# Retention followed by mixture of depths: when the second and third batch's tokens are chosen, and how the first MLPs are dealt out to the steps

## Chip, cores, metric

One core of one Trainium2 chip. The metric is the device time of one execution in microseconds; the runs of the kernel before took 259.76 us in the median of three (258.28 to 263.15).

## The reference, cut to what matters

All arrays are float32. There are 8 batches of 8 heads, 576 positions and head size 64, so a token has 512 channels; the MLP has 1024 hidden units and each batch sends its 128 best tokens through it.

```python
scores = scale * np.matmul(q, k.transpose(0, 1, 3, 2))
gamma = 1.0 - 2.0 ** (-5.0 - np.arange(H))
Dmat = np.where(rel >= 0, gamma[:, None, None] ** rel[None, :, :], 0.0)
x = np.matmul(scores * Dmat, v)                 # to (B, S, H*D)
s = np.einsum('bsd,d->bs', x, w_gate)
out = x.copy()
for b in range(B):
    top_idx = np.argpartition(-s[b], capacity)[:capacity]
    xe = x[b, top_idx]
    ye = np.maximum(xe @ w1, 0.0) @ w2
    g = 1.0 / (1.0 + np.exp(-s[b, top_idx]))
    out[b, top_idx] = xe + g[:, None] * ye
```

## The kernel before

**Steps.** A batch has nine chunks of 64 positions. Two chunks make a page of q, k (both turned), v and k, 1 MB in four transfers, and there are 36 pages. Turn s of the main loop works on page s: `block(s)` writes to TensorE's queue the products of k and q of page s (`scores`, L184), the running state (`update`, L174, which reads `vs`, v scaled by the decay) and, for page s-1, the outputs (`crosswise`, L195 and L205, which reads the masked scores `am` of page s-1). A state update of the page's own first chunk stands in the last quarter of the block's order, and the outputs of page s-1 are dealt two by two between the other products, so a wait for `vs` or `am` stops everything behind it. `masked(s)` (VectorE, L260) then makes `am`, `values(s-1)` (VectorE, L269 and L278) the outputs and their gate scores, and `store(s-1)` (GpSimd queue, L286) writes them to memory. `scaled(s+1)` makes the next `vs`: on GpSimd (L160, one instruction), or on ScalarE (L156, eight) where `by_act` says so, and for page 12 on VectorE.

**Choosing tokens.** A batch ends with a page; `ends[b]` is the step in which its last values are made: 5, 9, 14, 18, 23, 27, 32, 36. After it, `total` (TensorE L311, ScalarE L315) sums a token's scores, `spread` (TensorE L326, ScalarE L331) lays them in a row on all partitions, five `compare` (VectorE L339) count for each token those ahead of it (its rank), `one_hot` (VectorE L352) turns ranks into a selection, `rows` (TensorE L360, ScalarE L363) turns that into row numbers, and `gather` (GpSimd L369) fetches the 128 rows from the output in memory. `turn` (TensorE L395, ScalarE L396) transposes them, `gates` (VectorE L386, ScalarE L387) makes the sigmoid. 

**The MLP** is cut into 16 parts: eight `up` (TensorE L404, ReLU on ScalarE L406) and eight `down` (TensorE L412), the last of which adds the result to the tokens (VectorE L417) and scatters them (GpSimd L418). `mlp(b)` appends the parts of a batch to a list, and `some(n)` issues the next n of it.

**The order is written out by hand.** Every engine runs its instructions in the order of the program. `plan` puts a call into one of the lists `mid`, `early` or `late` of a step. In a step the order is: `scaled(s+1)`, `block(s)`, `masked(s)`, list `mid`, `values(s-1)`, stores, list `early`, then `some(share[s])`, then list `late`. `share` is how many parts a step gets from the loop; it is computed from `start`, the steps in which the MLPs of the batches begin.

**Loads.** SP's queue brings pages and weights in program order, with four to six transfers in flight (`bring`, L92). In step 7 it is given, in this order: the first half of w1, page 9, the second half of w1, page 10, the first half of w2 (`lower`), pages 11 and 12, the second half of w2, pages 13 and 14. There are eight page buffers.

## Time and profile before

| what | value |
|---|---|
| median of the runs | 259.76 us (258.28 to 263.15) |
| the profiled execution, its own time | 259.35 us |
| its span, first to last instruction | 257.6 us |
| TensorE matmuls busy | 222.1 us (86%) |
| TensorE weight loads busy (beside the matmuls) | 174.4 us (68%) |
| VectorE, ScalarE, GpSimd busy | 130.4, 73.1, 96.5 us |
| mean TensorE clock granted | 0.985 |
| DMA | 56.56 MB, 220 GB/s over the span |
| chain that ended last, by engine | TensorE 61%, DMA 23%, issue 11% |

In the profile, PE is TensorE's matmuls, PEld its weight loads, DVE VectorE, ACT ScalarE, POOL GpSimd and SP the engine that issues the loads. L184 is line 184 of the kernel. "Issue" as a releaser means that the engine waited for nothing that the profile shows. A bracket behind a row of the timeline is the idle time before it and what ended that. A float32 matmul leaves two records, so an up part is 8 records and a down part 2.

### The profile page before, as it was taken

How to read it: one execution, taken by the hardware profiler on the slowest of the kernel's cores; microseconds unless marked ns; L12 is line 12 of the kernel's file. 1: busy time of each engine (PE TensorE's matmuls, PEld its weight loads, DVE VectorE, ACT ScalarE, POOL GpSimd, SP SyncE). 2: the span in 40 equal slices, each digit the busy share in tenths (PEclk: the TensorE clock that was granted, in tenths of full speed). 3: DMA queues.
4: the chain of work that ended last, by engine and by line, in shares of the span. 5: the costliest groups of instructions: out<-in, count | busy, mean ns of one | idle time of the engine just before them, and what ended most of it. 6: DMA issues, size and time to landing. Idle time of an engine off the chain costs nothing.

```text
span 257.6 us, 11547 instructions
## 1 busy us (share of the span) xinstructions
PE 222.1 (86%) x5147; PEld 174.4 (68%) x5147; DVE 130.4 (51%) x355; ACT 73.1 (28%) x255; POOL 96.5 (37%) x132
## 2 busy tenths in 40 slices
PE   0875775897884999999999799999999999999991
PEld 0864564894563797689758796698669966874950
DVE  0164795339543359358535396569235774650201
ACT  2121563322011145133412234235122442221200
POOL 4313811181173460843175514550546422301101
PEclk9999999999799899999999999999999999999999
DMA  5887988989999988887889977998323304201101
GB/s 190 271 272 235 314 305 289 343 290 403 296 303 340 294 266 276 249 316 266 255 294 296 323 244 238 349 305 291 116 46 101 68 5 125 74 11 41 41 0 41
DMA packets 28097, 56.56 MB, mean 220 GB/s; under 512 B 4112, under 2 KB 4240, under 8 KB 28048
## 3 DMA queue, kind: packets, MB, share of 16 engines
q1 hardware_dynamic: 23184, 42.19, 49.9%
q0 software_dynamic: 4864, 13.64, 16.3%
q8 instruction: 40, 0.66, 1.1%
q14 instruction: 9, 0.07, 0.1%
HBM read 44.28 MB, written 11.53 MB: 217 GB/s over the span
## 4 chain that ended last, share of the span: by engine, by line
PE 61%; DMA 23%; issue 11%; ACT 1%; POOLq 1%; SPq 1%; POOL 0%; ACTq 0%
DMA raw<-in_qkvk 19%; PE h_ps L404 18%; PE ye_ps L412 18%; PE sc_ps L184 8%; PE u_ps L174 7%; DMA w_sb<-in_w 4%; PE y_ps L195 3%; PE y_ps L205 3%; PE row_ps L326 2%; PE xg_ps L395 1%; SPq L92 1%; ACT vs L156 1%; PE rs_ps L311 1%; POOLq L602 1%; PE idx_ps L360 1%
## 5 line engine op out<-in xcount | busy, mean ns | idle before, releaser
L260 DVE TENSOR_TENSOR am<-sc_ps,table 128x512 f32<-128x512 f32 x36 | 24.9, 690 | 80.6 <-PE sc_ps L184 65.8
L404 PEld LDWEIGHTS h_ps<-xg,w_sb 128*128 128x128 f32 x512 | 59.9, 193 | 6.5 <-issue 4.4
L404 PE MATMUL h_ps<-xg,w_sb 128*128 128x128 f32 x512 | 62.8, 279 | 1.3 <-ACT xg L396 0.7
L412 PE MATMUL ye_ps<-w_sb,hT 128*128 128x512 f32 x128 | 61.9, 617 | 0.2 <-issue 0.2
L184 PE MATMUL sc_ps<-raw 64*64 64x64 f32 x1152 | 47.2, 227 | 14.6 <-DMA raw<-in_qkvk 8.5
L184 PEld LDWEIGHTS sc_ps<-raw 64*64 64x64 f32 x1152 | 41.2, 141 | 16.5 <-DMA raw<-in_qkvk 8.6
L286 POOL DMA_DIRECT2D out<-xs x64 | 39.2, 620 | 31.0 <-DVE xs L269 30.8
L214 ACT COPY st<-u_ps 128x256 f32<-128x256 f32 x64 | 23.8, 371 | 93.5 <-PE u_ps L174 49.2
L174 PE MATMUL u_ps<-vs,raw 64*64 64x64 f32 x1024 | 44.6, 228 | 5.0 <-ACT st L214 3.0
L195 PE MATMUL y_ps<-vs,am 64*64 64x64 f32 x1152 | 46.8, 226 | 2.1 <-issue 1.4
L174 PEld LDWEIGHTS u_ps<-vs,raw 64*64 64x64 f32 x1024 | 37.2, 140 | 12.5 <-issue 4.9
L160 POOL TENSOR_TENSOR vs<-raw,table 128x512 f32<-128x512 f32 x27 | 28.3, 1049 | 39.9 <-DMA raw<-in_qkvk 39.6
L205 PE MATMUL y_ps<-st,raw 64*64 64x64 f32 x1024 | 39.0, 223 | 4.9 <-issue 4.9
L195 PEld LDWEIGHTS y_ps<-vs,am 64*64 64x64 f32 x1152 | 39.4, 137 | 3.4 <-issue 2.3
L339 DVE SCALAR_TENSOR_TENSOR scr<-row,rs,ahead 128x576 f32<-128x576 f32 (+5 forms) x47 | 34.2, 727 | 8.9 <-ACT row L331 6.2
L205 PEld LDWEIGHTS y_ps<-st,raw 64*64 64x64 f32 x1024 | 35.0, 139 | 5.3 <-issue 5.3
L412 PEld LDWEIGHTS ye_ps<-w_sb,hT 128*128 128x128 f32 x128 | 23.0, 194 | 21.4 <-issue 20.1
L278 DVE SCALAR_TENSOR_TENSOR scr<-xs,table 128x256 f32<-128x256 f32 x72 | 31.0, 430 | 2.5
L406 ACT ACTIVATE hT<-h_ps 128x128 f32<-128x128 f32 x64 | 17.5, 276 | 45.1 <-PE h_ps L404 43.1
L369 POOL DMA_INDIRECT xr<-out,idx x8 | 8.1, 1016 | 55.6 <-ACT idx L363 55.6
L269 DVE TENSOR_TENSOR xs<-y_ps,table 128x512 f32<-128x512 f32 (+1 forms) x37 | 24.7, 667 | 5.6 <-PE y_ps L205 5.6
L418 POOL DMA_INDIRECT out<-o,idx x8 | 9.5, 1186 | 25.8 <-DVE o L417 24.8
(38 smaller groups left out, 108.9 us busy)
## 6 DMA issues: line engine op xcount, KB each, us to landing
raw<-in_qkvk SPq DMA_DIRECT2D x144, 256.0 KB
out<-xs POOLq DMA_DIRECT2D x64, 128.0 KB, 5.2
w_sb<-in_w SPq DMA_DIRECT2D x16, 256.0 KB
out<-xs POOLq DMA_DIRECT2D x16, 64.0 KB, 4.8
table<-in_consts SPq DMA_DIRECT2D x1, 234.5 KB
xr<-out,idx POOLq DMA_INDIRECT x8, 4.3
out<-o,idx POOLq DMA_INDIRECT x8, 3.0
```

Of the source, the lines that this page charges most:

```text
L160: engine.tensor_tensor(out=blocks(vs[s]), in0=blocks(raw[s][:, 2, :]), in1=dec[:, 0, HH * c : HH * c + H].unsqueeze(2).to_broadcast([P, H, ...
L174: yield lambda h=h, half=half: nc.tensor.matmul(u_ps[b][half, where(0, h)], raw[s][half, 3, where(e, h)], vs[s][half, where(e, h)], start= ...
L184: yield lambda e=e, h=h, half=half: nc.tensor.matmul(sc_ps[s][half, where(e, h)], raw[s][half, 1, where(e, h)], raw[s][half, 0, where(e, h ...
L195: yield lambda e=e, h=h, i=i, half=half: nc.tensor.matmul(y_ps[s][halves[1 - i], where(e, h)], am[s][half, where(e, h)], vs[s][half, where ...
L205: yield lambda g=g, e=e, h=h, i=i, half=half: nc.tensor.matmul(y_ps[s][halves[1 - i], where(e, h)], raw[s][half, 0, where(e, h)], st[g - 1 ...
L260: nc.vector.tensor_tensor(out=blocks(am[s]), in0=blocks(sc_ps[s]), in1=causal.unsqueeze(1).to_broadcast([P, H, C]), op=OP.mult)
L269: nc.vector.tensor_tensor(out=blocks(xs[s])[:, i0:i1, :], in0=blocks(y_ps[s])[:, i0:i1, :], in1=dec[:, 1, HH * c + i0 : HH * c + i1].unsqu ...
L278: nc.vector.scalar_tensor_tensor(scr, xs[s][:, W * e : W * e + W], 1.0, wgh, op0=OP.mult, op1=OP.mult, accum_out=sc[b][:, c : c + 1])
L286: nc.gpsimd.dma_start(out=outs[b][C * c : C * c + 2 * C, W * i : W * i + W] .rearrange("(c p) d -> p c d", c=2), in_=xs[s][half, :].rearra ...
L339: nc.vector.scalar_tensor_tensor(scr[:n, : j1 - j0], row[b][:n, j0:j1], rs[b][:n, k : k + 1], ahead[:n, at + j0 : at + j1], op0=OP.subtrac ...
L404: nc.tensor.matmul(t[:, a, :], w1_sb[:, d, P * (f + a) : P * (f + a) + P], xg[b][:, d, :], start=d == 0, stop=d == KD - 1)
L412: nc.tensor.matmul(ye[b], hT[b][:, a, :], w2_sb[:, a, :], start=a == 0, stop=a == FB - 1)
```

## The change

The numbers of steps are those of `ends` above.

- First batch: four parts in step 8 as before, then four in each of steps 9 and 10 (they were three each), two ahead of the second batch's `turn` in step 11 and two behind it. Its gates move from step 11 to step 8.
- Second w2 half: loaded before page 12, no longer after it.
- Second batch (b = 1): `total`, `spread` and the compares in step 9 (total was there; spread and compares were in step 10). The compares are in the list `late` of step 9, so they stand ahead of the mask of page 10 on VectorE. `one_hot` in step 10, `rows` and `gather` at the end of step 10, followed by `scaled(11)` and the store of page 9; `turn` in step 11 (was 13), gates in step 12 (was 13).
- `scaled(12)` goes back to GpSimd at the usual place; `scaled(11)` is the one moved behind the gather.
- Third batch (b = 2): `spread` and compares in step 14 (were in 15), `one_hot` in 15 (was 16), `rows` and `gather` in the list `early` of step 16, ahead of that step's two parts (they were behind its three), `turn` in step 17 (was 18). `scaled(17)` moves from ScalarE to GpSimd, in the usual place ahead of block 16.
- Parts issued in steps 8 to 22: before 4, 3, 3, 2, 2, 4, 3, 3, 3, 3, 4, 4, 4, 4, 4; after 4, 4, 4, 6, 3, 2, 3, 2, 2, 3, 4, 3, 3, 3, 4.
- Stores of pages 10 and 15 move to match.

```diff
-    by_act = lambda s: ends[0] <= s < ends[0] + 3 or s - 3 in ends[2:-1]
+    by_act = lambda s: ends[0] <= s < ends[0] + 3 or s - 3 in ends[3:-1]
...
-            AHEAD + 4: [(lower, FB // 2)]}
+            AHEAD + 3: [(lower, FB // 2)]}
...
-    plan(late, s + 5, gates, 0)
-    start = [s + 2]
+    plan(late, s + 2, gates, 0)
+    start = []
     for b in range(1, last):
         s = ends[b]
-        plan(late, s, total, b)
-        plan(early, s + 1, spread, b, columns(0, full), columns(full, NK))
-        for k in range(NK):
-            plan(late, s + 1, compare, b, k)
-        plan(mid, s + 2, one_hot, b)
-        if b > 1:
-            plan(mid, s + 2, scaled, s + 3)
-        plan(late, s + 2, rows, b)
-        plan(late, s + 2, gather, b)
-        if b == 1:
-            plan(late, s + 2, store, s)
-            plan(late, s + 2, scaled, s + 3, nc.vector)
-        plan(late, s + 2, store, s + 1)
-        plan(early, s + 4, turn, b)
-        plan(early, s + 4, mlp, b)
-        plan(late, s + 4, gates, b)
-        start.append(s + 4)
+        if b < 3:
+            plan(early, s, some, 2)
+            plan(early, s, total, b)
+            plan(early, s, some, 1)
+            plan(early, s, spread, b, columns(0, full), columns(full, NK))
+            for k in range(NK):
+                plan(late, s, compare, b, k)
+            plan(mid, s + 1, one_hot, b)
+            plan(late, s + 3, gates, b)
+        if b == 1:
+            plan(early, s, some, 1)
+            plan(early, s + 1, some, 4)
+            plan(late, s + 1, rows, b)
+            plan(late, s + 1, gather, b)
+            plan(late, s + 1, scaled, s + 2)
+            plan(late, s + 1, store, s)
+            plan(early, s + 2, some, 2)
+            plan(early, s + 2, turn, b)
+            plan(early, s + 2, mlp, b)
+            plan(early, s + 2, some, 4)
+        elif b == 2:
+            plan(early, s + 2, rows, b)
+            plan(early, s + 2, gather, b)
+            plan(early, s + 2, store, s + 1)
+            plan(early, s + 3, some, 1)
+            plan(early, s + 3, turn, b)
+            plan(early, s + 3, mlp, b)
+            plan(early, s + 3, some, 2)
+            start.append(s + 3)
+        else:
...
-    share = {}
+    share = {ends[1] + 3: 3}
+    share.update({x: 2 for x in (ends[1] + 4, ends[2] + 1, ends[2] + 2)})
     for i, (s0, s1) in enumerate(zip(start, start[1:])):
-        left, s = 2 * FB - 2, s0
-        if i == 0:
-            left, s = left - 4, s0 + 1
+        left, s = (2 * FB - 2, s0) if i else (2 * FB - 3, s0 + 1)
...
-    stores[AHEAD + 2] = ()
+    stores[AHEAD + 2] = stores[ends[2] + 2] = ()
...
-        if s + 1 < NS and not by_act(s + 1) and s != ends[1] + 2:
+        if s + 1 < NS and not by_act(s + 1) and s != ends[1] + 1:
             scaled(s + 1)
...
-                    if x - 1 not in ends[1:last]:
+                    if x - 1 not in ends[3:last]:
                         store(x)
```

What stands behind `else:` for the later batches is the old text, unchanged.

More of the change, by code (lines that the diff above doesn't have):

```diff
@@ L147, with scaled @@
     vs, am, sc_ps, y_ps, u_ps, st, xs, sc = {}, {}, {}, {}, {}, {}, {}, {}
-    by_act = lambda s: ends[0] <= s < ends[0] + 3 or s - 3 in ends[2:-1]
-    def scaled(s, engine=nc.gpsimd):
+    by_act = lambda s: ends[0] <= s < ends[0] + 3 or s - 3 in ends[3:-1]
+    def scaled(s):
         c = batch(2 * s)[1]
@@ L159, in scaled @@
             return
-        engine.tensor_tensor(
+        nc.gpsimd.tensor_tensor(
             out=blocks(vs[s]), in0=blocks(raw[s][:, 2, :]),
@@ L507 @@
     plan(late, s, gate_vector)
-    plan(late, s + 5, gates, 0)
-    start = [s + 2]
+    plan(late, s + 2, gates, 0)
+    start = []
     for b in range(1, last):
         s = ends[b]
-        plan(late, s, total, b)
-        plan(early, s + 1, spread, b, columns(0, full), columns(full, NK))
-        for k in range(NK):
-            plan(late, s + 1, compare, b, k)
-        plan(mid, s + 2, one_hot, b)
-        if b > 1:
-            plan(mid, s + 2, scaled, s + 3)
-        plan(late, s + 2, rows, b)
-        plan(late, s + 2, gather, b)
-        if b == 1:
-            plan(late, s + 2, store, s)
-            plan(late, s + 2, scaled, s + 3, nc.vector)
-        plan(late, s + 2, store, s + 1)
-        plan(early, s + 4, turn, b)
-        plan(early, s + 4, mlp, b)
-        plan(late, s + 4, gates, b)
-        start.append(s + 4)
+        if b < 3:
[28 more added lines that the diff above has]
+        else:
+            plan(late, s, total, b)
+            plan(early, s + 1, spread, b, columns(0, full), columns(full, NK))
+            for k in range(NK):
+                plan(late, s + 1, compare, b, k)
+            plan(mid, s + 2, one_hot, b)
+            plan(mid, s + 2, scaled, s + 3)
+            plan(late, s + 2, rows, b)
+            plan(late, s + 2, gather, b)
+            plan(late, s + 2, store, s + 1)
+            plan(early, s + 4, turn, b)
+            plan(early, s + 4, mlp, b)
+            plan(late, s + 4, gates, b)
+            start.append(s + 4)
```

## The prediction, made before the changed kernel was run

> **What bounds the kernel now.** I read the page first, then TensorE's waits, then busy time by stage, then the timelines of TensorE, VectorE and GpSimd around steps 8 to 18. Step s below is turn s of the main loop; its mask (L260) dates it: step 9 at 52.25 us, 11 at 67.08, 13 at 77.79, 18 at 110.64.

> Page, part 2, shares of a slice (6.44 us) in tenths:

> ```profile
> ## 2 busy tenths in 40 slices
> PE   0875775897884999999999799999999999999991
> ...
> PEclk9999999999799899999999999999999999999999
> DMA  5887988989999988887889977998323304201101
> ```

> TensorE is full from the 14th slice (83.7 us) almost to the end. Before it DMA is full and TensorE has holes, the deepest in the 13th slice (4), and its clock sags behind them (7 in the 11th, 8 in the 14th). TensorE's waits from 36 to 126 us (total, times, longest):

> ```profile
> PE y_ps L205 <- issue: 4.2, 2, 3.5
> PE sc_ps L184 <- DMA raw<-in_qkvk: 2.4, 1, 2.4
> ```

> Two holes matter. Stages (columns: window, its length, busy time and count per engine, clock, DMA share, GB/s):

> ```profile
> core 0: us, PE busy (x) PEld busy (x) DVE busy (x) ACT busy (x) POOL busy (x), PEclk, DMA share, GB/s
> 62.38:65.80 3.42, 1.06 (x60) 0.95 (x64) 1.96 (x6) 0.37 (x1) 0.00 (x0) 0.99 1.00 365
> 65.80:69.20 3.40, 3.36 (x85) 2.54 (x75) 2.09 (x5) 0.37 (x1) 1.04 (x1) 0.51 0.88 262
> ...
> 79.45:82.86 3.41, 1.14 (x8) 0.88 (x8) 0.74 (x2) 0.18 (x1) 0.95 (x1) 0.99 0.95 350
> 82.86:86.28 3.42, 3.42 (x8) 1.74 (x7) 1.22 (x5) 0.40 (x1) 1.32 (x3) 0.51 0.87 273
> 86.28:126.00 39.72, 39.23 (x1003) 32.88 (x1003) 26.89 (x71) 15.08 (x56) 17.09 (x22) 1.00 0.85 276
> ```

> Each hole is followed by 3.4 us at half clock. TensorE's timeline shows the price; a pair of down parts (x4 records, L412) is 1.88 us at full clock:

> ```profile
> 68.16 2.46 PE L412 MATMUL ye_ps<-w_sb,hT 128*128 128x512 f32 x4
> ...
> 81.72 0.33 PE L205 MATMUL y_ps<-st,raw 64*64 64x64 f32 x3 [3.51 <-issue]
> ...
> 82.47 3.28 PE L412 MATMUL ye_ps<-w_sb,hT 128*128 128x512 f32 x4
> 85.55 2.28 PE L404 MATMUL h_ps<-xg,w_sb 128*128 128x128 f32 x16
> ...
> 111.50 1.88 PE L412 MATMUL ye_ps<-w_sb,hT 128*128 128x512 f32 x4
> ```

> The first hole (63.05 to 65.36) is page 11's keys. The second is nobody's: "issue". At 79.5 the trace has one 16 KB packet of the instruction queue, and TensorE goes on 1.3 us after its end, so I read it as a late instruction fetch; the queue's line is

> ```profile
> q8 instruction: 40, 0.66, 1.1%
> ```

> After 86.28 TensorE is 99% busy up to 126 and 95% to 180, so from 65 on the end moves by what TensorE saves or loses.

> [...] 0.51 for 3.4 us behind two windows in which TensorE was busy 1.1 us. [...] 10,294 matmuls and weight loads over 40 packets is 257. [...] the timelines show program order. [...] gathers, from the end of their issue:

> ```profile
> DMA to landing us min/median/max: 3.4/4.3/5.2
> ```

> **The change part by part.** Unit prices, all from the trace: block of a step 2.09 us (98.14 to 100.23), up 0.95 (8 records), down 0.94, turn 0.66, total 0.28, spread 0.85, index matmuls 0.2. Five compares, and the mask behind them:

> ```profile
> 60.14 0.82 DVE L339 SCALAR_TENSOR_TENSOR scr<-row,rs,ahead 128x576 f32<-128x576 f32 x1
> ...
> 64.33 0.07 DVE L339 DVE_READ_ACCUMULATOR scr<-row,rs,ahead 64x1 f32 x1
> 67.08 0.69 DVE L260 TENSOR_TENSOR am<-sc_ps,table 128x512 f32<-128x512 f32 x1 [2.67 <-PE sc_ps L184]
> 67.69 0.88 DVE L352 TENSOR_TENSOR hot<-slots,rank 128x512 f16<-128x512 f32 x2
> ```

> so 4.26 us, starting 0.5 after spread's end (59.6 to 60.14).

> No TensorE work is added or dropped. Parts of MLPs done by the end of steps 8 to 13 were 4, 7, 10, 12, 14, 18; now 4, 8, 12, 18, 21, 23; both reach 46 at step 21. Only what is placed ahead of a hole is a gain.

> *Step 9.* Block ends 53.2 as before; two ups 55.1, total 55.4, up 56.3, spread 57.1, up 58.1. Compares 57.6 to 61.9, mask of 10 to 62.5, one-hot to 63.4, values of 9 to 65.0. Their delay costs nothing here: the mask is first read in block 11, at 65. Without that cover it would be 4.3 us.
> *Step 10.* Block to 60.2, four downs. Rows 2 and 3 of w2 have landing records at 62.8 and 63.7, so downs end 64.8; index 65.0. Block 11's first quarter runs to 65.5, and keys landed 65.2: the first hole is gone. Gain: two downs and the index, 2.1. With it goes the half clock: downs 2.46-1.88 = 0.6, block's last three quarters 2.87-1.57 = 1.3. Together 4.0.
> *Step 11.* GpSimd now issues gather 1 (1.03 us) ahead of the scaled values of 11 (1.04), moved here from before block 10. Index matmuls to gather took 0.66 (70.62 to 71.28): gather 65.5 to 66.5, values to 67.6; the block's last quarter wants them at 66.6: stall 1.0. Block ends 68.2, downs 4 and 5 70.1 (w2's second half takes page 12's place, first rows landed 67.1). Gather lands 66.5 plus 4.3 to 5.2, I take 4.9: 71.4. The transposes wait 1.2 (0.7 to 1.6), and the four parts behind them wait too. Two downs, two ups: step 12 begins near 75.9. The gather's other condition, batch 1's output in memory, is met: its last store landed at 64.2. GpSimd's queue goes on: store of 9 (two at 0.62, was in step 11), scaled 12 (was VectorE's; waits for page 12, below, to 75), store of 10, scatter 0 (1.2; batch 0's sum is ready at 74.9), scaled 13 to 77.6, wanted at 82: nothing on the path.
> *Page 12* moves 1 MB back; landings ran 3.3 us per MB (page 11's values 66.0, page 13's 75.8), so its values come at 69 + 3.3 plus 1.6 for the gather and a store now ahead: 74. Block 12's scores start at 76.4: nothing. Behind it SP's queue is as before, so page 13 keeps its time and block 13 comes later (80.8 for 76.1). Block 14 comes earlier (84.8 for 87.8), but its scaled values started at 81.9 and are wanted at 86: nothing.
> *The second hole*: the code between fetches differs (step 11 is now 10 us long), so I take this stall as gone: 3.5, and its half clock, 3.28-1.88 + 2.28-1.95 = 1.7. Together 5.2. This is the least certain term: from 0 gained (it comes again in full) to 5.2.
> *Steps 14 and 15.* Spread ends at T. Compares T+0.5 to T+4.75, mask of 15 to T+5.4. TensorE: block 15, two downs, block 16's cross half at T+4.0, which reads that mask: stall 1.45. Waiting behind it: all of block 16. This is the ranks-ahead-of-masks price where only two parts cover it.
> *Steps 16 and 17.* VectorE: one-hot T+6.2, values of 14 written T+6.9; GpSimd: store of 14 (two at 0.62) to 8.2, scaled 17 (1.05, was ScalarE's) to 9.3, gather to 10.3, landing 14.6 to 15.5. TensorE: block 16 ends T+7.55, index 0.2, two downs, block 17, one down: T+12.7. Transposes wait 1.9 to 2.8, I take 2.2.
> *The rest*: gates 0 and 2 earlier, values of 12 off VectorE (0.69), 8 ScalarE copies (2.02) dropped: those engines are 30 to 60% idle from 86 to 126; nothing. SP's queue: only page 12 and w2 swap.

> Sum: 4.0 + 5.2 - 1.0 - 1.2 - 1.45 - 2.2 = 3.35 gained. The profiled execution took 259.35 (span 257.6, 1.75 around it), so 256.0; the median of runs is 259.76, 0.4 above: 256.4.

> **Rivals.** *A, as summed*, 256.4, its own range 255.2 to 257.8.
> *B, the fetch stall stays.* For: steps 12 to 16 are 4 to 5 us for some 270 instructions, the density at which it came, and DMA is 85 to 93% busy. Against: by then six loads in flight give way to four, and most fetches before cost nothing. A small one, as at 146.5 (1.36), gives 257.8; the whole 5.2 gives 261.6, slower than before. It decides from 3.35 up.
> *C, transposes hardly wait.* Gathers at their shortest (3.4) take 1.2 and 1.5 off the two waits, 253.7; with block 11's stall smaller too, 252.8 to 255.2. For: 3.4 was measured; against: that was in the quiet end, those in busy stretches took 4 to 5.2.
> *D, no more than a shift.* Page 12 is late and TensorE waits in block 12 instead: needs 2.4 us beyond my 74; a third microsecond on top and half clock give 259 to 260.

> **How the numbers follow.** A 0.48, B 0.25 (evenly from 257.8 to 261.6), C 0.21, D 0.06. The range 253.4 to 260.6 leaves out B's end and C's low end. Faster by over 2% (under 254.6; 2% is about what a measurement of this kernel tells from no change) is most of C, 0.16; slower (over 265) needs several stalls, 0.03; within 0.81.

> **What would show it.** Right: no half-clock window between 62 and 72; block 11 starts by 65.1 without a DMA wait; waits of turn on the gather of 1 to 2 us in steps 11 and 17; block 16 waits on L260 1.4 us. Wrong: an "issue" wait of over 1 us between 70 and 105, or TensorE waiting for page 12.

## Result, and the profile after

| | before | after |
|---|---|---|
| median of 22 runs each, same chip | 259.64 us (254.63 to 263.23) | 261.82 us (258.18 to 270.0) |
| profiled execution, its own time | 259.35 us | 262.99 us |
| its span | 257.6 us | 261.2 us |
| mean TensorE clock | 0.985 | 0.974 |

The ratio is 1.0116, with 95% interval 1.0068 to 1.0165: the changed kernel is about 1% slower, where I had 256.4 us and a range of 253.4 to 260.6. The ratio compares the executions within 1.5% of the fastest of the same kernel, so it isn't quite that of the two medians. Two repeats gave 1.0041 (1.0002 to 1.0079) and 1.0075 (0.9971 to 1.0178).

Page, part 2, of the changed kernel (a slice is 6.53 us):

```profile
## 2 busy tenths in 40 slices
PE   0867784899969998699999999999999998999991
...
PEclk9997999599999999979999999999999999999999
DMA  5878989999999887977989986987223304201101
```

The deep hole of the 13th slice is gone (9 for 4). A new dent stands in the 17th slice (6, from 104.5 us), with a clock of 7 in the 18th; and the clock sags early, to 5 in the 8th slice (45.7 to 52.2 us). TensorE's waits of the changed kernel from 36 to 126 us (total, times, longest):

```profile
PE xg_ps L395 <- DMA xr<-out,idx: 3.9, 2, 2.1
PE sc_ps L184 <- issue: 2.5, 1, 2.5
...
PE y_ps L195 <- DVE am L260: 1.3, 1, 1.3
```

Both waits that the change was priced on are gone: no row for page 11's keys, none of 3.5 us on "issue". In their place stand the transposes behind two gathers and block 16 behind its mask. On TensorE's timeline of the changed kernel:

```profile
75.37 0.63 PE L395 MATMUL xg_ps<-eye,xr 128*128 128x128 f32 x4 [1.77 <-DMA xr<-out,idx]
...
100.67 0.27 PE L195 MATMUL y_ps<-vs,am 64*64 64x64 f32 x2 [1.30 <-DVE am L260]
...
110.77 0.98 PE L395 MATMUL xg_ps<-eye,xr 128*128 128x128 f32 x4 [2.10 <-DMA xr<-out,idx]
111.55 1.91 PE L412 MATMUL ye_ps<-w_sb,hT 128*128 128x512 f32 x2
```

The last two rows show the half clock that a new wait brings: turn takes 0.98 instead of 0.66, one down part (x2) 1.91 instead of 0.94. The stages (length, busy times, clock) of the changed kernel: an early one, the one in which the first hole was, and the one behind the second gather's wait:

```profile
49.50:52.93 3.43, 3.43 (x18) 3.43 (x17) 0.00 (x0) 0.56 (x2) 2.85 (x5) 0.50 1.04 362
...
62.38:65.80 3.42, 3.42 (x89) 2.34 (x80) 3.31 (x9) 0.74 (x2) 0.00 (x0) 1.00 0.95 315
...
110.96:114.37 3.41, 3.41 (x12) 2.35 (x12) 0.88 (x2) 0.59 (x1) 0.00 (x0) 0.50 0.79 295
```

The first hole's window is full (3.42 of 3.42, for 1.06) at full clock, and so is the second's (3.38 of 3.41 at 79.45). 10.2 us of half clock stand elsewhere: two windows from 46.1 us and one behind the gather.

**Where the time went.** The stretch from the mask of page 8 to that of page 22 holds the whole change; the same number of MLP parts is done at its end. It took 90.23 us before and 93.57 after, 3.34 more, and the two own times differ by 3.64. Cut at the mask of page 14, before:

```profile
45.53:88.96 43.43, 35.87 (x839) 27.86 (x833) 20.61 (x55) 8.97 (x29) 18.88 (x26) 0.92 0.94 324
88.96:135.76 46.80, 45.84 (x1179) 36.25 (x1172) 28.19 (x76) 15.92 (x57) 20.65 (x28) 1.00 0.85 276
```

and after:

```profile
45.71:89.98 44.27, 40.17 (x859) 33.26 (x849) 20.82 (x53) 10.42 (x34) 19.91 (x27) 0.92 0.94 327
89.98:139.28 49.30, 44.19 (x1141) 33.27 (x1142) 28.52 (x76) 12.91 (x44) 21.84 (x29) 0.97 0.84 277
```

Length less PE's busy time is TensorE's idle time: 7.56 before and 4.10 after in the first part, 0.96 and 5.11 in the second. Idle moved, in sum 8.52 to 9.21. Busy time for the same work rose from 81.71 to 84.36. A part of that is the clock: the four up parts of step 8 took 6.21 us at half clock, for 3.84 before.

One execution isn't a typical one here, so I took three profiles of each kernel (page 8's mask to page 22's, us):

| profile | stretch | idle to 14, after 14 | busy | half clock | largest waits |
|---|---|---|---|---|---|
| before | 90.23 | 7.56, 0.96 | 81.71 | 6.8 | keys 2.36, issue 3.51 |
| before, second | 88.29 | 6.66, 1.81 | 79.83 | 3.4 | pages 1.44, 1.80; vs 1.02 |
| before, third | 88.08 | 7.48, 0.00 | 80.60 | 6.8 | pages 1.11, 1.99; issue 2.93 |
| after | 93.57 | 4.10, 5.11 | 84.36 | 10.2 | gathers 1.77, 2.10; mask 1.30 |
| after, second | 92.22 | 5.76, 5.42 | 81.04 | 3.4 | vs 1.75; gathers 2.41, 2.29; mask 1.30 |
| after, third | 87.03 | 2.57, 3.87 | 80.59 | 1.8 | gathers 0.71, 1.17; mask 1.30 |

On average idle went from 8.15 to 8.94 and busy from 80.7 to 82.0: 2.1 us longer, about what the runs say. Three profiles are few, and the chips differ: the second and third of before come from a chip on which it took 256 us, those of the changed kernel from chips on which before took 260. Only the first of each share a chip.

### The profile page after: what moved, and what is told of

Its sections match the earlier page's. It is cut to its first block, busy times and chain, and to the rows that moved or that the text cites. A ratio compares the mean times of both kernels' runs of the same rounds, so it can differ in the third digit from the quotient of the medians.

```text
span 261.2 us, 11542 instructions
## 1 busy us (share of the span) xinstructions
PE 226.4 (87%) x5147; PEld 178.0 (68%) x5147; DVE 131.3 (50%) x354; ACT 71.7 (27%) x247; POOL 98.9 (38%) x134
## 4 chain that ended last, share of the span: by engine, by line
PE 56%; DMA 20%; issue 12%; DVE 5%; ACT 2%; POOL 2%; POOLq 1%; SPq 1%; DVEq 0%; ACTq 0%
PE h_ps L404 18%; PE ye_ps L412 14%; DMA raw<-in_qkvk 9%; PE sc_ps L184 7%; PE u_ps L174 6%; DMA xr<-out,idx 5%; DMA w_sb<-in_w 4%; DVE scr L339 4%; PE y_ps L205 3%; PE y_ps L195 3%; DMA out<-xs 2%; PE row_ps L326 2%; PE xg_ps L395 2%; POOL vs L160 1%; SPq L92 1%
## 5 line engine op out<-in xcount | busy, mean ns | idle before, releaser
L404 PEld LDWEIGHTS h_ps<-xg,w_sb 128*128 128x128 f32 x512 | 62.6, 200 | 6.7 <-issue 3.8
L404 PE MATMUL h_ps<-xg,w_sb 128*128 128x128 f32 x512 | 65.9, 286 | 1.2 <-ACT xg L396 0.7
L412 PE MATMUL ye_ps<-w_sb,hT 128*128 128x512 f32 x128 | 61.5, 611 | 0.8 <-issue 0.5
L260 DVE TENSOR_TENSOR am<-sc_ps,table 128x512 f32<-128x512 f32 x36 | 24.8, 690 | 73.5 <-PE sc_ps L184 63.4
L184 PE MATMUL sc_ps<-raw 64*64 64x64 f32 x1152 | 47.5, 228 | 11.4 <-DMA raw<-in_qkvk 7.0
L195 PE MATMUL y_ps<-vs,am 64*64 64x64 f32 x1152 | 47.7, 227 | 4.2 <-issue 2.2
L184 PEld LDWEIGHTS sc_ps<-raw 64*64 64x64 f32 x1152 | 41.5, 142 | 13.8 <-issue 6.4
L195 PEld LDWEIGHTS y_ps<-vs,am 64*64 64x64 f32 x1152 | 40.2, 138 | 5.6 <-issue 2.9
L160 POOL TENSOR_TENSOR vs<-raw,table 128x512 f32<-128x512 f32 x29 | 30.7, 1060 | 29.7 <-DMA raw<-in_qkvk 19.4
L339 DVE SCALAR_TENSOR_TENSOR scr<-row,rs,ahead 128x576 f32<-128x576 f32 (+5 forms) x47 | 34.2, 727 | 14.3 <-ACT row L331 11.6
L205 PE MATMUL y_ps<-st,raw 64*64 64x64 f32 x1024 | 39.1, 222 | 1.1 <-issue 0.9
L412 PEld LDWEIGHTS ye_ps<-w_sb,hT 128*128 128x128 f32 x128 | 22.6, 192 | 20.7 <-issue 19.7
L205 PEld LDWEIGHTS y_ps<-st,raw 64*64 64x64 f32 x1024 | 35.1, 138 | 1.5 <-issue 1.2
L278 DVE SCALAR_TENSOR_TENSOR scr<-xs,table 128x256 f32<-128x256 f32 x72 | 32.3, 448 | 2.5
L369 POOL DMA_INDIRECT xr<-out,idx x8 | 8.2, 1019 | 52.4 <-ACT idx L363 52.2
L417 DVE SCALAR_TENSOR_TENSOR o<-ye_ps,gate,xr 128x512 f32<-128x512 f32 x8 | 6.0, 751 | 31.7 <-PE ye_ps L412 31.7
## 6 DMA issues: line engine op xcount, KB each, us to landing
raw<-in_qkvk SPq DMA_DIRECT2D x144, 256.0 KB, 4.8
w_sb<-in_w SPq DMA_DIRECT2D x16, 256.0 KB, 5.1
```

The source lines that it names most:

```text
L160: nc.gpsimd.tensor_tensor(out=blocks(vs[s]), in0=blocks(raw[s][:, 2, :]), in1=dec[:, 0, HH * c : HH * c + H].unsqueeze(2).to_broadcast([P, ...
L184: yield lambda e=e, h=h, half=half: nc.tensor.matmul(sc_ps[s][half, where(e, h)], raw[s][half, 1, where(e, h)], raw[s][half, 0, where(e, h ...
L195: yield lambda e=e, h=h, i=i, half=half: nc.tensor.matmul(y_ps[s][halves[1 - i], where(e, h)], am[s][half, where(e, h)], vs[s][half, where ...
L205: yield lambda g=g, e=e, h=h, i=i, half=half: nc.tensor.matmul(y_ps[s][halves[1 - i], where(e, h)], raw[s][half, 0, where(e, h)], st[g - 1 ...
L260: nc.vector.tensor_tensor(out=blocks(am[s]), in0=blocks(sc_ps[s]), in1=causal.unsqueeze(1).to_broadcast([P, H, C]), op=OP.mult)
L278: nc.vector.scalar_tensor_tensor(scr, xs[s][:, W * e : W * e + W], 1.0, wgh, op0=OP.mult, op1=OP.mult, accum_out=sc[b][:, c : c + 1])
```

## Experiments

My first theory was that the waits priced at 1.0, 1.2, 1.45 and 2.2 us are real and that the second hole isn't gained; the rivals, that the half clock behind the new waits does it, or that one of the change's two parts does. Kernels of a group ran on one chip, beside the kernel before. Diffs are against the changed kernel unless it says otherwise.

**Group 1, one part alone** (before: 256.09 us here).

*before_again*: the kernel before, once more.

> The kernel before, unchanged, for a second profile of it. If the fetch hole near 78 us (3.5 us) and the half clock behind it belong to the kernel, they come again at the same place. If they are chance of one execution, this profile has neither, its span is some 5 us shorter than 257.6 unless another hole comes, and my term of 5.2 us for their loss was never there to gain.

Measured 252.7 us, span 251.0. The second hole isn't there. TensorE's timeline of this run:

```profile
76.32 0.27 PE L184 MATMUL sc_ps<-raw 64*64 64x64 f32 x2 [1.80 <-DMA raw<-in_qkvk]
78.50 0.37 PE L174 MATMUL u_ps<-vs,raw 64*64 64x64 f32 x2 [1.02 <-POOL vs L160]
```

In its place TensorE waits for page 13 and its scaled values (and 1.44 us for page 11 at 65.23, for 2.36), and its idle time over the stretch is 8.46 us where it was 8.52. Still, it reached the mask of page 14 in 40.90 us after that of page 8, for 43.43; the rest took 47.39, for 46.80, with an "issue" wait of 0.90 in it. Its own 252.7 us can't be set against the first profile's 259.35, which is of another chip; executions of the same kernel beside it took 252.43 to 258.99.

*second_batch_only*: the third batch's part undone. By a slip in my table of parts, two that should have been issued in step 18 were left to the end of the program, where the last stage (from the mask of page 35) grew from 44.6 to 46.3 us.

```diff
-        if b < 3:
+        if b == 1:
...
-    share = {ends[1] + 3: 3}
-    share.update({x: 2 for x in (ends[1] + 4, ends[2] + 1, ends[2] + 2)})
+    share = {12: 3, 13: 2, 14: 2, 15: 2, 16: 2, 17: 1}
```

> The change without its third-batch part (third batch chosen and transposed as before; parts of steps 14 to 17 are 2, 2, 2, 1 so that step 18 starts with the same 30 parts done as before). Theory, new waits: in the changed kernel the mask behind the third batch's compares costs 1.3 us, its transposes wait 2.1 us for the gather and bring a half-clock window (about 1.7 us); without them the time is 3.5 to 5 us below the changed kernel, ratio to before 0.99 to 1.0. Rival, the first MLP's four parts a step and the second batch cost it: ratio stays at 1.01.

Measured 255.87 us, 1.0051 (0.9969 to 1.0132): not told from no change, with the slip in it. The mask wait is gone; the first gather's is 2.12, values of 11 0.77.

*third_batch_only*: the kernel before with the third batch's part, three parts covering its compares.

```diff
         s = ends[b]
+        if b == 2:
+            plan(early, s, some, 2)
...
+    share[14] -= 3
+    share[17] -= 3
```

> The kernel before with only the third-batch part of the change (third batch's spread and compares in step 14, index and gather early in step 16, transposes in step 17; steps 15 and 16 have three parts each, one more cover than in the changed kernel). Theory, new waits: mask wait about 0.4 us, transposes wait about 1.2 us, with half clock in some runs; ratio to before 1.005 to 1.015. Rival, the first part of the change is to blame: ratio 1.000 within 0.003.

Measured 255.97 us, 1.0056 (0.9978 to 1.0134): no gain and no loss that the runs resolve. Its later waits: 0.98 for the gather, 1.16 on "issue" in block 15. Up to the mask of page 14 TensorE has the same work as in the kernel before, so this is a fourth profile of that stage. It has no second hole either (its largest wait there is 1.58 for a page). From the mask of page 8 to that of page 14, without the hole (this one, then before_again) and with it (before_third_profile, below), in the columns of the stages above:

```profile
46.44:85.86 39.42, 33.39 (x839) 26.34 (x835) 20.71 (x54) 8.97 (x29) 18.03 (x25) 1.00 0.96 327
...
45.12:86.02 40.90, 34.24 (x839) 27.14 (x835) 20.61 (x54) 8.97 (x29) 18.03 (x25) 0.96 0.94 324
...
45.05:87.97 42.92, 35.44 (x839) 27.59 (x835) 21.39 (x54) 9.08 (x29) 18.54 (x26) 0.92 0.94 320
```

The two executions with the hole needed 42.92 and 43.43 us, the two without 39.42 and 40.90. Half clock in the stage was 6.8 us in the first two, none and 3.4 in the others.

*second_turn_behind_downs*: in step 11 all four downs stand ahead of `turn`.

```diff
-            plan(early, s + 2, some, 2)
+            plan(early, s + 2, some, 4)
             plan(early, s + 2, turn, b)
             plan(early, s + 2, mlp, b)
-            plan(early, s + 2, some, 4)
+            plan(early, s + 2, some, 2)
```

> The changed kernel, only with the second batch's transposes behind all four remaining down parts of the first in step 11, in place of between them. Theory, new waits: the wait for the gather (1.8 us in the profile of the changed kernel) is covered by two downs (1.9 us) and goes; 1.5 to 2 us below the changed kernel, ratio to before about 1.004. Rival, this wait only took the place of one that comes anyway (page, fetch): no difference from the changed kernel, 1.01.

Measured 258.05 us, 1.009 (0.9993 to 1.0187). The wait for the first gather is gone as meant; mask 1.30 and second gather 2.23 stay, and "issue" took 2.14 in step 20. One wait taken away isn't seen in the time.

**Group 2, the later waits** (before: 260.16).

*after_again*: the changed kernel, 22 runs.

> The changed kernel, unchanged, for a second profile and on one chip with the next three. Theory now: the fetch hole of before was chance (its second profile has none and 252.7 us), so the sum of my prediction without its 5.2 us, 1.85 us slower, is what remains: ratio 1.007 to 1.012, waits of 1.3 us on the mask before block 16 and about 2 us on the gather in step 17. Rival, chance of the clock in the first profile: ratio within 0.004 of 1.

Measured 262.41 us, 1.0041 (1.0002 to 1.0079).

*third_turn_a_step_later*: the third batch's `turn` goes back to step 18.

```diff
-            plan(early, s + 3, some, 1)
-            plan(early, s + 3, turn, b)
-            plan(early, s + 3, mlp, b)
             plan(early, s + 3, some, 2)
+            plan(early, s + 4, turn, b)
+            plan(early, s + 4, mlp, b)
+            plan(early, s + 4, some, 1)
```

> The changed kernel, only with the third batch's transposes in step 18 as before (step 17 has two parts, step 18 one more behind them); its choice stays a step sooner. Theory, the wait for the gather and the half clock behind it are the larger half of the loss: the 2.1 us wait and up to 2 us of half clock go, 2 to 4 us below the changed kernel, ratio to before 0.995 to 1.003; the mask wait of 1.3 us stays. Rival, the mask and the thinner steps cost it: less than 1 us off.

Measured 262.71 us, 1.0116 (1.0036 to 1.0197). The second gather's wait is gone in the trace, and from mask 14 to 22 took 46.7 us (49.3, 48.2 and 46.2 in the three profiles of the changed kernel), but the time isn't better: a miss.

*three_parts_of_cover*: three parts instead of two behind the third batch's compares.

```diff
-    share = {ends[1] + 3: 3}
-    share.update({x: 2 for x in (ends[1] + 4, ends[2] + 1, ends[2] + 2)})
+    share = {12: 2, 13: 1, 15: 3, 16: 3}
```

> The changed kernel with two parts moved later: steps 12 and 13 have 2 and 1 parts (were 3 and 2), steps 15 and 16 have 3 each (were 2). No work is added; from step 11 on TensorE is full, so moving the parts costs nothing by itself. Theory, cover: the mask wait falls from 1.3 to 0.4 us and the gather's from 2.1 to about 1.2, the half-clock window behind it is less likely: 2 to 3.5 us below the changed kernel. Rival, waits only move (steps 12 and 13 get thin and meet a late page or fetch): no difference, ratio 1.008 to 1.012.

Measured 262.27 us over 22 runs, 1.0078 (1.0031 to 1.0126): a miss too. A late row of TensorE's timeline says why:

```profile
128.67 3.44 PE L412 MATMUL ye_ps<-w_sb,hT 128*128 128x512 f32 x4 [2.65 <-issue]
```

The mask wait is gone and the second gather's is 0.42, but "issue" stalls of 1.37, 1.86 and 2.65 us came in steps that had none, and one of 1.77 us for rows of w1 in step 9.

*filler_in_third_wait*: two matmuls more ahead of the third `turn`, whose output nobody reads. They keep TensorE busy in the wait and compute nothing of the result.

```diff
             plan(early, s + 3, some, 1)
+            plan(early, s + 3, filler)
             plan(early, s + 3, turn, b)
```

> The changed kernel with two added matmuls of a down part's shape pair (128 x 128 by 128 x 512, 0.94 us each, into a bank that nobody reads) in step 17 ahead of the third batch's transposes, in the time in which TensorE waits for the gather. Theory, half clock: the wait takes 0.2 us instead of 2.1, no time is lost, and the half-clock window behind it (1.0 us on the downs and 0.6 us on the ups in the changed kernel's profile) is gone: 0 to 2 us below the changed kernel, by how often it came. Rival, the wait alone costs: equal to the changed kernel, or up to 1 us above it.

Measured 264.91 us, 1.0103 (1.0003 to 1.0203): the wait is filled, no half clock follows it, and nothing is gained. Half clock behind the second gather isn't needed for the loss: the second and third profile of the changed kernel have none there either.

**Group 3, the waits together** (before: 255.8).

*second_only_turn_behind_downs*: the first and last edit of group 1 together, with the same slip.

> Second-batch part of the change alone, with the second batch's transposes behind all four down parts in step 11; third batch as before. Theory, new waits: the wait of 1.8 to 2.4 us for gather 1 goes and nothing takes its place; 1 to 3 us below before, ratio 0.988 to 0.996. Rival, the early stage is bound by DMA and by fetches whatever the order of the parts: ratio 1.000 within 0.004.

Measured 257.99 us (251.59 to 262.83), too wide for an interval; nothing follows.

*third_ranks_split*: two compares ahead of the mask of page 15, three behind it.

```diff
             for k in range(NK):
-                plan(late, s, compare, b, k)
+                if b == 2 and k > 1:
+                    plan(mid, s + 1, compare, b, k)
+                else:
+                    plan(late, s, compare, b, k)
```

> The changed kernel with two of the third batch's five compares ahead of the mask of page 15 and three behind it. Theory, waits in a chain: the mask wait before block 16 (1.30 us in four profiles of it) goes to zero, block 16 runs 1.3 us sooner, but the index and the gather stay where VectorE and GpSimd put them, so the wait of the transposes in step 17 grows from 2.1 to about 3.3: time as the changed kernel, ratio to before 1.006 to 1.012, half clock behind the wait more often. Rival, the waits are separate: 1.3 us below the changed kernel and a gather wait of 2.1 as before.

Measured 260.73 us, 1.0183 (1.0134 to 1.0232). The mask wait is gone. TensorE's timeline:

```profile
108.22 1.11 PE L395 MATMUL xg_ps<-eye,xr 128*128 128x128 f32 x4 [4.03 <-DMA xr<-out,idx]
```

The gather's wait grew from 2.1 to 4.0, with half clock behind it (1.11 for 0.66): mask and gather are one chain, and what is taken from its first link reaches the second.

*all_waits_covered*: the split, `turn` of the second batch behind four downs, and `turn` of the third in step 18.

> The changed kernel with three edits: second batch's transposes behind all four down parts in step 11, the third batch's compares split two and three around the mask of page 15, and its transposes and gates in step 18 as before (step 17 one part, step 18 six). Theory: no TensorE wait over 0.8 us on a gather or a mask from step 11 to 18; against the changed kernel 1.8 + 1.3 + 2.1 us and some half clock less, 4 to 6 us, ratio to before 0.985 to 0.995. Rival, the waits stand in for page and fetch waits that come anyway: less than 2 us below the changed kernel, ratio 1.000 to 1.008.

Measured 255.54 us over 22 runs, 0.9978 (0.9896 to 1.0059). No loss is left that the runs resolve; the changed kernel itself was not run on this chip. The largest wait left after block 8 is

```profile
69.00 0.27 PE L174 MATMUL u_ps<-vs,raw 64*64 64x64 f32 x2 [2.15 <-POOL vs L160]
```

the values of 11 behind the gather on GpSimd.

*before_third_profile*: the kernel before, once more.

> The kernel before once more, one look. If the 3.5 us fetch hole in block 13 is chance, it is not here; page waits in steps 11 to 14 together of 3 to 5 us are, as in the second profile of it.

Measured 256.34 us, with the second hole back at its old place:

```profile
80.79 0.34 PE L205 MATMUL y_ps<-st,raw 64*64 64x64 f32 x3 [2.93 <-issue]
```

**Group 4, against the last wait** (before: 260.02).

*after_same_chip*: the changed kernel.

> The changed kernel on one chip with the next two. Ratio to before 1.004 to 1.012 as in the two comparisons so far; mask wait 1.3 us, gather waits of 1.5 to 2.4 us in steps 11 and 17.

Measured 264.0 us, 1.0075 (0.9971 to 1.0178).

*all_covered_values_on_vector*: all_waits_covered, with the scaled values of 11 on VectorE.

```diff
-            plan(late, s + 1, scaled, s + 2)
+            plan(late, s + 1, scaled, s + 2, nc.vector)
```

> all_waits_covered, with the scaled values of page 11 made on VectorE (0.69 us) in place of behind gather 1 on GpSimd. Theory, waits: the wait for them in block 11 (0.8 to 2.15 us in the profiles) goes too; against the changed kernel on this chip 4 to 6 us less, ratio to before 0.985 to 0.996. Rival, fetch stalls and pages set the pace of steps 8 to 22 and every wait taken away comes back as one of those: ratio 0.997 to 1.004, only what the added waits of the changed kernel cost is won back.

Measured 258.48 us (252.31 to 265.03), no interval. The wait for `vs` is gone.

*second_only_covered*: the second batch's part alone, its two early waits covered (`turn` behind four downs, values of 11 on VectorE), and the slip of group 1 mended.

```diff
-        if b < 3:
+        if b == 1:
...
-            plan(late, s + 1, scaled, s + 2)
+            plan(late, s + 1, scaled, s + 2, nc.vector)
             plan(late, s + 1, store, s)
-            plan(early, s + 2, some, 2)
+            plan(early, s + 2, some, 4)
...
+    share = {12: 3, 13: 2, 14: 2, 15: 2, 16: 2, 17: 1, 18: 2}
```

> Second-batch part alone, transposes behind the four downs, scaled values of page 11 on VectorE, and the two parts of step 18 that second_batch_only and its follower left to the end put back. Theory, waits: as all_covered_values_on_vector, since the third batch's part by itself moves no work ahead of a hole: the two within 0.4%, both under before by 1%. Rival as there: ratio 0.997 to 1.004.

Measured 256.66 us, 0.9881 (0.9819 to 0.9942): faster than the kernel before in this comparison of six runs, and the profile has no half clock at all in the stretch. The stretch takes 86.84 us, and its largest wait after block 8 is

```profile
107.99 0.66 PE L395 MATMUL xg_ps<-eye,xr 128*128 128x128 f32 x4 [1.04 <-DMA xr<-out,idx]
```

**Group 5, is it the third part?** (before: 255.88).

*second_covered_third_as_changed*: the changed kernel with the two early waits covered, its third batch as it is.

```diff
-            plan(late, s + 1, scaled, s + 2)
+            plan(late, s + 1, scaled, s + 2, nc.vector)
...
-            plan(early, s + 2, some, 2)
+            plan(early, s + 2, some, 4)
```

> The changed kernel with only the second batch's waits taken away (transposes behind the four downs, scaled values of page 11 on VectorE); its third-batch part uncovered, as the change has it. Beside second_only_covered it is the price of the third-batch part. Theory: mask 1.3 us, gather 1.2 to 2.3 us and at times half clock (about 1.7 us), so 3 to 5 us above second_only_covered, ratio to before 0.998 to 1.008. Rival, the third part is harmless and the second batch's waits were the whole loss: within 1 us of second_only_covered, ratio 0.986 to 0.994.

Measured 257.3 us over 22 runs, 0.9986 (0.9927 to 1.0046). In its profile the mask cost 0.75 us and the second gather nothing; an "issue" stall of 1.67 us stands in block 17, ahead of it.

*second_only_covered_again*:

> second_only_covered, unchanged, as the partner of second_covered_third_as_changed on its chip. Theory: ratio to before 0.984 to 0.994 as in its first comparison (0.988). Rival, that was chance: 0.996 to 1.004.

Measured 255.35 us (250.57 to 257.28), no interval. Its profile has no half clock in the stretch either, but waits 1.51 us for rows of w2 in step 10 and 1.17 on "issue" in block 13. By the medians the third part costs 2 us on top; the runs don't resolve it, and on this chip the gain over before is 0.5 us instead of 3.

## Why the prediction was wrong, step by step

**The waits added (1.0, 1.2, 1.45, 2.2): right in kind and about in size.** In the three profiles of the changed kernel the mask of 15 cost 1.30 each time; the second gather 2.10, 2.29, 1.17; the first 1.77, 2.41, 0.71; the values of 11 nothing, 1.75 and 0.23. I had 5.85 us in all; the profiles give 5.2, 7.8 and 3.4. My 4.9 us for a gather was near by luck. The line that I took it from, 3.4/4.3/5.2, counts from the start of the issue and not from its end, and covers two gathers of the eight, neither of these two. By the times of the semaphores that TensorE waits for, the second and third batch's gathers landed 5.1 and 5.3 us after the end of their issue in the first profile of before, and 6.1 and 4.9, 6.0 and 5.1, 4.3 and 3.9 in the three of the changed kernel.

second_only_covered, with none of these waits (1.04 for the third batch's gather, in step 18) and without the third part, stands 1.0075 - 0.9881 = 1.9% below the changed kernel beside it, though that 1.0075 is open from 0.9971 to 1.0178. Rival C, transposes that hardly wait, fell.

**The first hole (2.1): gone, as I said.** No profile of the changed kernel waits for page 11's keys. The step fell late in the profiled one (the mask of 10 at 65.46, not 62.5): TensorE was 3 us behind from step 8, where four up parts that the change doesn't touch ran at half clock behind the 2.50 us stall at 45.05.

**Page 12 (rival D): harmless**, as I said; nothing waited for it.

**The second hole's 3.5 of waiting: gone in the changed kernel, but not a fixture of the kernel before.** No profile of the changed kernel has an "issue" wait of 1 us between block 8 and mask 22, so rival B's stall isn't what slowed it. Up to mask 14 its idle time other than the new waits is 2.3, 1.6 and 1.6 us; in the first profile of before it was 1.7 other than the two holes. But I had taken the hole from one execution. Two of four profiles of that stage have it, and those with it are 2.0 to 4.0 us longer, not 5.2. What goes there isn't all gained either: in second_only_covered neither hole stands as it was and one wait of 1.04 is added, so by my prices its idle time was due at some 4 us (8.52 - 5.6 + 1.0); its two profiles have 6.05 and 9.19.

**The half clock (1.9 in the 4.0, 1.7 in the 5.2): the step that failed.** The sum has two kinds of terms. In idle time I had 2.1 + 3.5 gone and 5.85 added, so 0.25 more; the first profiles show 0.69 more and the means of three 0.79. That part came out, on average. In busy time I had 1.9 + 1.7 = 3.6 us saved, all of it half clock. This was more than the whole gain of 3.35, and it didn't come: busy time rose, by 2.65 us in the first profiles and by 1.3 in the means. Two errors are in the term:

- The half clock didn't go. It left both old places, but I charged none to the new waits, and none to the stall ahead of block 8. The stretch has 10.2, 3.4 and 1.8 us of it after, 6.8, 3.4 and 6.8 before. Twice the mean clock's shortfall times the span, over all executions of group 2, gives 12.6 us (standard error 1.2) for after_again and 16.6 (1.0) for before: 4.0 less, where I had 6.8 less.
- It was priced too high. I charged 3.6 us for 6.8 us of it. Over the 16 profiles that do the same parts in the stretch (all but the filler and the two with the slip in group 1 and 3) a straight line through busy time against half-clock time has a slope of 0.33 (standard error 0.06). The four profiles of one code up to mask 14 agree: busy 35.87 and 35.44 us with 6.8 of half clock, 34.24 with 3.4, 33.39 with none. So the 4.0 us that went are worth about 1.3 us (an estimate from that slope), not 3.6.

The sum without the 5.2 is 4.0 - 1.0 - 1.2 - 1.45 - 2.2 = -1.85, slower by 1.85 us, and the medians say 2.2. That is partly luck: it leaves out 3.5 us of waiting that did go and keeps 1.9 of half clock that didn't. second_only_covered shows the same error by itself. Neither of the two holes nor any half clock is in its stretch in that profile, and hardly a wait is added; by my prices it was due about 8 us (9.2 less the 1.04 for a gather). It gained 0.0119 x 260 = 3.1 us on one chip and 0.5, by the medians, on the other.

**Odds.** All but one of the signs that I had named came true in the first profile: no half clock between 62 and 72, block 11 without a DMA wait, transposes waiting 1.77 and 2.10 us, block 16 1.30, no "issue" wait over 1 us between 70 and 105. Only block 11 began late, at 67.55 and not by 65.1. The time was longer all the same, since no sign looked at half clock outside the two old places. I gave slower than before only the upper half of B and a part of D. The sign of the sum hung on terms taken from a single profile; a second one would have shown the hole missing and the stage to mask 14 shorter by 2.5 us without any change.

**What the change is worth in its parts.** The second batch's earlier choice brings work ahead of a hole, and with its gather and its values covered it was faster in one of two comparisons. The third batch's part brings none: from mask 14 to mask 22 TensorE was idle for 0.00 to 1.81 us before and for 3.87 to 5.42 after. It adds a chain of mask and gather, and moving one link handed the wait to the next.

**Open.** At equal half clock the 12 profiles with the second batch's part hold 1.1 us (standard error 0.35) more busy time in the stretch than the four without it; why isn't shown. Whether the third part costs its 2 us is not resolved by its own pair. Why single waits taken away (third_turn_a_step_later, three_parts_of_cover) left the time alone is shown for the second, "issue" stalls, and not for the first, which had none. Seven of the 15 profiles with the second batch's part have a half-clock window that begins around the start of step 8 (45.1 to 48.0 us), and none of the four without it, though TensorE's code up to there is the same: chance isn't excluded.

## To carry to other kernels

Keep two sums, one of idle time and one of half clock, and ask of each new wait whether it brings half clock, as you ask of each old one whether it takes it along. Take two or three profiles of the kernel before: a stall may come and go by itself (the one of 3.51 us here was absent in two of four profiles), and then its full price doesn't belong in a sum. Moving a chain of choosing, gathering and transposing earlier left TensorE waiting here where the work between two links was shorter than the link: of the 5.5 us from the end of the third batch's spread (95.17) to block 16's use of the mask (100.67), 4.2 had work, and 1.30 were a wait; the second gather's wait was 1.17 to 2.29. Count that cover link by link, as a wait removed can move to the next: in third_ranks_split the mask's 1.30 us went, and the gather's wait grew from 2.1 to 4.0.
